# An adaptive-layernorm attention block: the gate's matmuls threaded into the K and V matmuls, and the scores placed ahead of V

## The chip, the core and the metric

The kernel runs on one core of a Trainium2 chip. The core has a matrix engine (TensorE, PE in the profile, with its weight loads listed apart as PEld), a vector engine (DVE), a scalar engine for activations (ACT), a general engine (POOL) and a synchronisation engine (SP) that issues most of the transfers. The engines run side by side, each through its own list of instructions in a fixed order, and wait for one another on semaphores. Matmuls write into eight accumulation banks (PSUM), from which DVE or ACT copy the results into the on-chip memory (SBUF). The metric is the device time of one execution in microseconds (us).

## What is computed

```python
def reference(x, c, wqkv, wo, w_mod):
    B, N, D = x.shape                      # 2, 256, 1152
    mod = (_silu(c) @ w_mod).reshape(B, 6, 1, D)
    shift_a, scale_a, gate_a, ... = [mod[:, i] for i in range(6)]
    h = _layernorm(x, axis=-1) * (1 + scale_a) + shift_a
    qkv = h @ wqkv
    q, k, v = ...
    p = _softmax(jnp.einsum('bqd,bkd->bqk', q, k) * D ** (-0.5), axis=-1)
    a = jnp.einsum('bqk,bkd->bqd', p, v) @ wo
    return x + gate_a * a
```

All tensors are bf16. Three of the six modulation vectors are used: shift, scale and gate. The gate multiplies the columns of the projected attention, so it can equally be multiplied into the columns of `wo`, once for each batch, and this kernel does that.

## The kernel before

The 512 rows (2 batches of 256) form four row tiles of 128, numbered 0 to 3; tiles 0 and 1 are batch 0, tiles 2 and 3 batch 1. The 1152 features form nine blocks of 128, numbered j. A small scheduler (`Sched`) notes what each operation reads and writes, derives the semaphore waits from that, and emits the operations of every engine in the order in which the program lists them. So the order of the lines is the order of each engine's queue, and nothing is reordered later. PSUM banks are handed out by `get_bank` (line 287), the least recently taken first; a matmul that starts in a bank waits until the bank's last contents have been read.

The stages, in the order of the program:

- Transfers: x, then the shift and scale columns of `w_mod` (tile `wmss`), the weights of Q, the gate columns (`wmg`), the weights of K, of V, and `wo` (into `woG[:, 0]`). All are issued at the start, nearly all from SP.
- Statistics and normalisation of x on DVE and ACT, while TensorE multiplies silu(c) (`cTs`, padded to 128 columns, two of which carry data) with `wmss`, in five chunks of up to 512 columns (`mod_ss_j`). Between those matmuls it transposes the normalised rows block by block (`xn_transposes_j`), through two banks in turn; every transposed block is copied to `hT[:, j]` by the engine that the list `raw_evict_eng` (line 475) names.
- The shift and scale rows are copied to `modsb` (line 488 on), transposed into columns by 18 transposes of two rows (line 496 on), and turned into per-partition scalars (`modT_group`), with which `modulate` (line 514) scales and shifts each block of `hT`.
- Q and K (`qk_group`, line 528): groups of five and four output blocks, each a bank that accumulates over nine matmuls of 512 columns. ACT copies them to `qkT`. Between them stand `mod_gate` (line 552), the gate's 27 matmuls in the same form as those for shift and scale, and `gate_bcast_and_woG` (line 561). This spreads each batch's gate row over all 128 partitions by multiplying with a selector (`sel`), copies the result to `gateb`, and has DVE multiply `wo` with it, first into `woG[:, 1]` and then in place in `woG[:, 0]`.
- V (`v_tile`, line 541): four row tiles, each in three banks (512, 512 and 128 columns); ACT copies them to `v_sb`.
- Attention: `scores`, `evict_scores` (ACT), `dve_chain` (scale, row maximum, subtraction), `exp_tile` (ACT), `finalize` (division by the row sum), `pT_of` (transposing the probabilities), `av_of` (attention times V, with the copies to `aT` alternating between ACT and DVE), and `proj`, which multiplies with `woG`, adds x on DVE and sends each chunk of the output off. The last lines (649 to 666) fix their order: scores of all four tiles with the softmax of batch 0 between them, then batch 0 up to its projection, then batch 1.

Before the loop over `xn`, a one-element `Exp` on ACT (line 453) brings in the exponential's table early.

Of the kernel before, what the change touches and what calls it, by code (L numbers as in the profile page):

```python
# [5 lines left out]
DT = mybir.dt  # L6
# [174 lines left out]
def bass_standalone__dit_adaln_block__diffusion_kernel(  # L181
# [70 lines left out]
    MPAD = 128  # L252
    cTs = salloc("cTs", [P, DC, MPAD], DT.bfloat16)
    modsb = salloc("modsb", [B, 3 * D], DT.bfloat16)
    modT = salloc("modT", [P, 2 * DC, B], DT.float32)
    onep16 = salloc("onep16", [P, DC, B], DT.bfloat16)
# [22 lines left out]
    pT = salloc("pT", [P, B, 2, N], DT.bfloat16, at=xn_off + 2 * NT * N * 2)  # L279
    assert 2 * NT * N * 2 + B * 2 * N * 2 <= NT * D * 2  # L280

    pb = [nc.alloc_psum_tensor(f"pb{i}", [P, 512], DT.float32) for i in range(8)]
    pb16 = [pb[i][:, :].bitcast(DT.bfloat16) for i in range(8)]

    lru = list(range(8))

    def get_bank(exclude=()):
        for i, b in enumerate(lru):
            if b not in exclude:
                lru.pop(i)  # L290
                lru.append(b)
                return b
        raise RuntimeError("no psum bank")

    def dma(dst, src, eng="sp", name=None):
# [3 lines left out]
    def mm(dst, lhsT, rhs, start, stop):  # L299
        return S.add("pe", lambda e: e.matmul(dst, lhsT, rhs, start=start, stop=stop),  # L300
                     reads=[lhsT, rhs], writes=[dst])

    def tp(dst, src, ident_ap):
        return S.add("pe", lambda e: e.transpose(dst, src, ident_ap),  # L304
                     reads=[src, ident_ap], writes=[dst])
# [51 lines left out]
    def alt(a="act", b="dve"):  # L357
        rr[0] ^= 1
        return a if rr[0] else b
# [28 lines left out]
    for k3 in range(3):  # L388
# [8 lines left out]
          reads=[ident[:]], writes=[ident[:]])  # L397
    S.add("pool", lambda e: e.memset(cTs[:], 0.0), writes=[cTs[:]])
    S.add("pool", lambda e: e.memset(sel[:], 1.0), writes=[sel[:]])
    S.add("pool", lambda e: e.affine_select(sel[:], sel[:], pattern=[[-1, B], [0, P]],  # L400
# [51 lines left out]
    act(xn[:, 3, :], xn[:, 3, :], ACT.Copy, scale_=rden[:, 3:4])  # L452
    act(rs1[:, 0:1], ve16[:, 0:1], ACT.Exp)
    for i in (0, 1, 2):
# [7 lines left out]
    def mod_ss_j(j):  # L462
        for k, (c0, w) in enumerate(ss_chunks):
            mm(pb[ss_banks[k]][0:MPAD, 0:w], cTs[:, j, :], wmss[:, j, c0:c0 + w],
               start=(j == 0), stop=(j == DC - 1))

    tp_banks = [get_bank(exclude=ss_banks), get_bank(exclude=ss_banks)]

    def xn_transposes_j(j, evict_eng):
# [3 lines left out]
        copy(evict_eng, hT[:, j, :], pb16[bk][:, 0:T])  # L473

    raw_evict_eng = ["dve", "dve", "act", "dve", "dve", "act", "dve", "dve", "act"]
    bk_w = get_bank(exclude=ss_banks)
# [5 lines left out]
    for kind, j in pre_order:  # L482
        if kind == "m":
            mod_ss_j(j)
        else:
            xn_transposes_j(j, raw_evict_eng[j])

    ev_order = [(0, "dve"), (2, "act"), (1, "act"), (3, "dve"), (4, "dve")]
    for k, eng in ev_order:
        c0, w = ss_chunks[k]  # L490
        copy(eng, modsb[0:2, c0:c0 + w], pb[ss_banks[k]][0:2, 0:w])

    xn_transposes_j(7, raw_evict_eng[7])
    JA = 3
    mps = {}
    for (j0, j1) in ((0, JA), (JA, DC)):
        bk_t = get_bank()
        n = j1 - j0
        view = pb16[bk_t][:, 0:2 * n * B].rearrange("p (m b) -> p m b", b=B)
        mps[(j0, j1)] = view  # L500
        for jj in range(j0, j1):
            for m, r in ((jj, jj - j0), (DC + jj, n + jj - j0)):
                tp(view[:, r, :], modsb[0:2, m * P:(m + 1) * P], ident[0:2, 0:2])
    xn_transposes_j(8, raw_evict_eng[8])

# [21 lines left out]

    def qk_group(t3, cols):
        banks = [get_bank() for _ in cols]
        for j in range(DC):  # L530
            for ci, cc in enumerate(cols):
                mm(pb[banks[ci]][:, 0:T],
                   wq[:, j, t3 * D + cc * P:t3 * D + (cc + 1) * P],
                   hT[:, j, :], start=(j == 0), stop=(j == DC - 1))
        for ci, cc in enumerate(cols):
            idx = t3 * DC + cc
            copy("act", qkT[:, idx, :], pb[banks[ci]][:, 0:T])

    v_chunks = [(0, 512), (512, 512), (1024, 128)]

    def v_tile(i):
        banks = [get_bank() for _ in v_chunks]
        for j in range(DC):
            for k, (c0, w) in enumerate(v_chunks):
                mm(pb[banks[k]][:, 0:w], hT[:, j, i * P:(i + 1) * P],
                   wq[:, j, 2 * D + c0:2 * D + c0 + w], start=(j == 0), stop=(j == DC - 1))
        for k, (c0, w) in enumerate(v_chunks):
            copy("act", v_sb[:, i, c0:c0 + w], pb[banks[k]][:, 0:w])

    g_chunks = [(0, 512), (512, 512), (1024, 128)]  # L550

    def mod_gate():
        banks = [get_bank() for _ in g_chunks]
        for j in range(DC):
            for k, (c0, w) in enumerate(g_chunks):
                mm(pb[banks[k]][0:MPAD, 0:w], cTs[:, j, :], wmg[:, j, c0:c0 + w],
                   start=(j == 0), stop=(j == DC - 1))
        for k, (c0, w) in enumerate(g_chunks):
            copy("dve", modsb[0:2, NSS + c0:NSS + c0 + w], pb[banks[k]][0:2, 0:w])

    def gate_bcast_and_woG():
        for b in range(B):
            gbanks = [get_bank() for _ in g_chunks]
            for k, (c0, w) in enumerate(g_chunks):
                mm(pb[gbanks[k]][:, 0:w], sel[:, b, :], modsb[0:2, NSS + c0:NSS + c0 + w],
                   start=True, stop=True)
            for k, (c0, w) in enumerate(g_chunks):
                copy("dve", gateb[:, b, c0:c0 + w], pb[gbanks[k]][:, 0:w])
        for b in (1, 0):
            gview = bass.AP(tensor=gateb, offset=b * D, ap=[[B * D, P], [0, DC], [1, D]])  # L570
            src = woG[:, 0, :, :]
            dst = woG[:, b, :, :]
            S.add("dve", lambda e, dst=dst, src=src, gview=gview: e.tensor_tensor(  # L573
                dst, src, gview, op=ALU.mult),
                  reads=[src, gateb[:, b, :]], writes=[dst])

    qk_group(0, [0, 1, 2, 3, 4])
    qk_group(0, [5, 6, 7, 8])
    mod_gate()
    qk_group(1, [0, 1, 2, 3, 4])  # L580
    gate_bcast_and_woG()
    qk_group(1, [5, 6, 7, 8])
    for i in range(NT):
        v_tile(i)

# [28 lines left out]

    def pT_of(b):
# [6 lines left out]
        copy("act", pT[:, b, 0, :], pb16[pt_banks[0]][:, 0:N])  # L622
        copy("dve", pT[:, b, 1, :], pb16[pt_banks[1]][:, 0:N])

    def av_of(b):
        for j in range(DC):
            bk = get_bank()
            for kt in range(2):
                mm(pb[bk][:, 0:N], v_sb[:, 2 * b + kt, j * P:(j + 1) * P],
                   pT[:, b, kt, :], start=(kt == 0), stop=(kt == 1))  # L630
            copy(alt(), aT[:, j, b * N:(b + 1) * N], pb[bk][:, 0:N])

# [3 lines left out]
    def proj(i, last=False):  # L636
        b, qt = divmod(i, 2)
        ob = outsb[:, i, :]
        for k, (c0, w) in enumerate(o_chunks):
# [24 lines left out]
    av_of(1)  # L664
    proj(2)
    proj(3, last=True)

# [30 lines left out]
```

## Time and profile before

| | us |
|---|---|
| median of six executions | 116.92 |
| lowest and highest of them | 115.56 and 118.42 |
| the profiled execution, its own time | 116.94 |
| its span, from the first to the last instruction | 115.2 |
| TensorE busy in the span | 101.6 |
| DVE busy | 54.2 |
| ACT busy | 37.3 |

The granted clock of TensorE over the span was 0.985 of full speed. In the profile, a row gives the source line, the engine, the operation, the tiles written and read, the shape, the number of instructions, and busy time and mean duration. Where a helper records an operation its line is the helper's: 300 is any matmul, 304 any transpose, 309 a copy on ACT, 311 a copy on DVE, 316 a DVE operation with a scalar. So the tiles' names tell the groups apart. A matmul's duration in a row is its latency; consecutive ones overlap, and their spacing has to be taken from the starts. The lists of waits name the instruction whose end released the waiting engine.

### The profile page before, as it was taken

The page shows a single profiled execution, that of the slowest core. Times are in us where ns is not written, and L with a number is a line of the kernel's source. Part 1 is how long each engine was busy: PE and PEld are TensorE (multiplying, and loading weights), DVE is VectorE, ACT ScalarE, POOL GpSimd, SP SyncE. Part 2 cuts the span into 40 slices and gives each one's busy share as a digit, 9 for nine tenths or more (in the row PEclk, how much of TensorE's full clock was granted, in tenths as well). Part 3 has the DMA queues.
Part 4 walks back from the last instruction along what each step waited for, and adds up shares of the span by engine and source line. Part 5 has one row for each costly group of instructions (what it writes and reads, how often), then busy time and mean ns, then how long its engine had stood idle before and what let it go on. Part 6 is the DMA issues. An engine that isn't in the chain of part 4 may idle for free.

```text
span 115.2 us, 1521 instructions
## 1 busy us (share of the span) xinstructions
PE 101.6 (88%) x596; PEld 52.3 (45%) x605; DVE 54.2 (47%) x142; ACT 37.3 (32%) x76; POOL 2.4 (2%) x10
## 2 busy tenths in 40 slices
PE   1728998939999999999989999999997899989990
PEld 1202445523444445544434445555575645574550
DVE  0369884699940000500099999000017577384332
ACT  2933694533008015000350073142157650051000
POOL 6100000000000000000000000000000000000000
PEclk9998699999999999999999999999999999999999
DMA  3999999999999999994000000000000001310131
GB/s 106 330 413 422 413 410 385 361 353 386 393 393 390 394 390 391 390 393 166 0 0 0 0 3 6 0 0 0 0 0 0 6 0 48 100 57 0 59 95 57
DMA packets 10811, 21.04 MB, mean 183 GB/s; under 512 B 1202, under 2 KB 4530, under 8 KB 10804
## 3 DMA queue, kind: packets, MB, share of 16 engines
q1 hardware_dynamic: 10368, 20.32, 48.0%
q10 hardware_dynamic: 436, 0.63, 1.5%
q8 instruction: 5, 0.08, 0.3%
q14 instruction: 2, 0.02, 0.0%
HBM read 19.76 MB, written 1.18 MB: 182 GB/s over the span
## 4 chain that ended last, share of the span: by engine, by line
PE 73%; DVE 9%; DMA 7%; ACT 5%; issue 1%; SPq 1%; DVEq 0%
PE pb L300 72%; DMA wmss<-in_w_mod_dram 7%; DVE hT L316 3%; ACT qkT L309 2%; PE pb L304 2%; DVE modsb L311 1%; ACT v_sb L309 1%; SPq L296 1%; DVE sc_92 L316 1%; DVE smax L339 1%; ACT pT L309 1%; DVE hT L311 1%; DVE outsb L322 1%; ACT hT L309 1%; ACT esb L334 0%
## 5 line engine op out<-in xcount | busy, mean ns | idle before, releaser
L300 PE MATMUL pb<-hT,wq 128*128 128x512 bf16 x159 | 35.5, 379 | 2.2 <-DVE hT L316 1.7
L300 PEld LDWEIGHTS pb<-hT,wq 128*128 128x128 bf16 x162 | 15.5, 98 | 21.2 <-DVE hT L316 2.5
L309 ACT ACTIVATE qkT<-pb 128x512 bf16<-128x512 f32 x18 | 9.2, 605 | 30.1 <-PE pb L300 30.1
L300 PE MATMUL pb<-wq,hT 128*128 128x512 bf16 (+1 forms) x106 | 17.6, 325 | 0.1
L300 PE MATMUL pb<-woG,aT 128*128 128x512 bf16 (+1 forms) x106 | 17.4, 325 | 0.1
L300 PE MATMUL pb<-wmss,cTs 128*128 128x512 bf16 (+1 forms) x44 | 11.2, 404 | 2.8 <-DVE stats L420 2.5
L300 PEld LDWEIGHTS pb<-woG,aT 128*128 128x128 bf16 x108 | 9.2, 98 | 8.5
L300 PEld LDWEIGHTS pb<-wq,hT 128*128 128x128 bf16 x108 | 9.1, 98 | 8.6
L573 DVE TENSOR_TENSOR woG<-woG,gateb 128x10368 bf16<-128x10368 bf16 x2 | 11.1, 5558 | 0.1
L322 DVE TENSOR_TENSOR outsb<-pb,xs 128x512 bf16<-128x512 f32 (+1 forms) x12 | 6.2, 553 | 8.3 <-PE pb L300 8.3
L311 DVE CAST modsb<-pb 2x512 bf16<-2x512 f32 (+2 forms) x6 | 3.1, 559 | 14.4 <-PE pb L300 14.4
L309 ACT ACTIVATE v_sb<-pb 128x512 bf16<-128x512 f32 (+1 forms) x12 | 5.0, 491 | 12.1 <-PE pb L300 12.1
L300 PEld LDWEIGHTS pb<-wmss,cTs 128*128 128x128 bf16 x45 | 4.4, 107 | 9.2 <-DVE stats L420 3.3
L316 DVE TENSOR_SCALAR sc_92<-sc_92 128x256 bf16<-128x256 bf16 x4 | 0.9, 222 | 14.1 <-ACT sc_92 L309 14.1
L311 DVE CAST gateb<-pb 128x512 bf16<-128x512 f32 (+1 forms) x6 | 2.9, 548 | 8.8 <-PE pb L300 8.8
L420 DVE BATCH_NORM_STATS2 stats<-xs 128x6 f32<-128x384 bf16 x9 | 4.4, 541 | 1.9 <-DMA xs<-in_x_dram 1.9
L300 PE MATMUL pb<-pT,v_sb 128*128 128x256 bf16 x36 | 4.3, 273 | 0.8 <-ACT pT L309 0.8
L316 DVE TENSOR_SCALAR hT<-hT,modT 128x256 bf16<-128x256 bf16 x18 | 4.8, 284 | 0.5
L334 ACT ACT_TABLE_LOAD x3 | 3.8, 1283 | 2.3 <-issue 2.2
L300 PE MATMUL pb<-wmg,cTs 128*128 128x512 bf16 (+1 forms) x26 | 4.5, 324 | 0.1
L311 DVE CAST aT<-pb 128x256 bf16<-128x256 f32 x9 | 3.8, 425 | 1.3 <-PE pb L300 1.2
L300 PE MATMUL pb<-qkT 128*128 128x256 bf16 x36 | 4.1, 272 | 0.0
(76 smaller groups left out, 65.4 us busy)
## 6 DMA issues: line engine op xcount, KB each, us to landing
wmss<-in_w_mod_dram SPq DMA_DIRECT2D x9, 576.0 KB, 10.1
wq<-in_wqkv_dram SPq DMA_DIRECT2D x6, 864.0 KB, 14.2
wmg<-in_w_mod_dram SPq DMA_DIRECT2D x3, 864.0 KB, 10.6
woG<-in_wo_dram SPq DMA_DIRECT2D x3, 864.0 KB, 14.0
wq<-in_wqkv_dram SPq DMA_DIRECT2D x3, 480.0 KB, 14.8
wq<-in_wqkv_dram SPq DMA_DIRECT2D x3, 384.0 KB, 9.5
out_dram<-outsb SPq DMA_DIRECT2D x8, 128.0 KB, 1.7
xs<-in_x_dram SPq DMA_DIRECT2D x2, 288.0 KB, 4.1
```

Of the source, the lines that this page charges most:

```text
L296: return S.add(eng, lambda e: e.dma_start(dst, src), reads=[src], writes=[dst], is_dma=True, own_sem_name=name)
L300: return S.add("pe", lambda e: e.matmul(dst, lhsT, rhs, start=start, stop=stop), reads=[lhsT, rhs], writes=[dst])
L304: return S.add("pe", lambda e: e.transpose(dst, src, ident_ap), reads=[src, ident_ap], writes=[dst])
L309: return S.add("act", lambda e: e.activation(dst, src, ACT.Copy), reads=[src], writes=[dst])
L311: return S.add(eng, lambda e: e.tensor_copy(dst, src), reads=[src], writes=[dst])
L316: return S.add(eng, lambda e: e.tensor_scalar(dst, src, a1, None, op0=op0), reads=rd, writes=[dst])
L322: return S.add(eng, lambda e: e.tensor_tensor(dst, a, b, op=op), reads=[a, b], writes=[dst])
L334: return S.add("act", lambda e: e.activation(dst, src, func, bias=bias, scale=scale_, accum_out=accum_out), reads=rd, writes=wr)
L339: return S.add(eng, lambda e: e.tensor_reduce(dst, src, axis=AX.X, op=op), reads=[src], writes=[dst])
L420: S.add("dve", lambda e, i=i, k3=k3: e.bn_stats(stats[:, i, k3, :], xs[:, i, k3 * LNC:(k3 + 1) * LNC]), reads=[xs[:, i, k3 * LNC:(k3 + 1) ...
L573: S.add("dve", lambda e, dst=dst, src=src, gview=gview: e.tensor_tensor(dst, src, gview, op=ALU.mult), reads=[src, gateb[:, b, :]], writes ...
```

## The change

The change has these parts.

- Bank bookkeeping: `mm` records which banks have an accumulation under way, and `get_bank` passes over those. `use_bank` takes a named bank; the transposes of shift and scale get two named ones.
- Start: other engines evict some transposed blocks (block 2 on DVE, block 7 on ACT), the copy of block 5 is put behind the copies of shift and scale, shift and scale are multiplied in the chunk order 0, 2, 1, 3, 4, and the transposes of block 7 come behind those of shift and scale. The one-element `Exp` moves behind Q's first group.
- Gate: 81 matmuls of two columns replace the 27. The stationary operand is now a 128x128 block of `wmg`, the moving one the two data columns of `cTs`, and one of them follows each of K's 81 matmuls. They give the gate as columns, in one bank (`bk_g`). `gate_finish` copies them to scalars and builds 18 tiles of 128x128 on DVE by adding a scalar to a zero tile `zt`; multiplying these with the identity spreads the gate (`gate_bcast_interleave`), threaded into V's second and third tile. `woG_scaling` follows V's third tile in the program.
- Attention: the scores of all tiles and the whole softmax stand ahead of V, in the tile order 2, 3, 0, 1. Batch 1 then goes first to its projection, with the copies of the probabilities and of `aT` on DVE alone, and batch 0 follows. The last output tile has four chunks (512, 256, 256, 128), sent from SP and ACT in turn.

```diff
@@ salloc
+    modsb_off = cursor[0]
     modsb = salloc("modsb", [B, 3 * D], DT.bfloat16)
+    gT16 = salloc("gT16", [P, DC, B], DT.bfloat16)
+    gT32 = salloc("gT32", [P, DC, B], DT.float32)
+    zt = salloc("zt", [P, P], DT.bfloat16)
...
+    gtile = salloc("gtile", [P, NGB, P], DT.bfloat16, at=modsb_off)
...
+    open_banks = set()
     def get_bank(exclude=()):
         for i, b in enumerate(lru):
-            if b not in exclude:
+            if b not in exclude and b not in open_banks:
...
+    S.add("pool", lambda e: e.memset(zt[:], 0.0), writes=[zt[:]])
...
-    act(rs1[:, 0:1], ve16[:, 0:1], ACT.Exp)
...
-        for k, (c0, w) in enumerate(ss_chunks):
+        for k in (0, 2, 1, 3, 4):
+            c0, w = ss_chunks[k]
...
-    raw_evict_eng = ["dve", "dve", "act", "dve", "dve", "act", "dve", "dve", "act"]
+    raw_evict_eng = ["dve", "dve", "dve", "dve", "dve", "act", "dve", "act", "act"]
...
-            xn_transposes_j(j, raw_evict_eng[j])
+            xn_transposes_j(j, raw_evict_eng[j], defer=(j == 5))
...
-    xn_transposes_j(7, raw_evict_eng[7])
+    flush_raw()
...
-        bk_t = get_bank()
+        bk_t = use_bank(bk_w if j0 == 0 else ss_banks[0])
...
+    xn_transposes_j(7, raw_evict_eng[7])
     xn_transposes_j(8, raw_evict_eng[8])
...
                 mm(pb[banks[ci]][:, 0:T], ...)
+                if interleave:
+                    interleave()
...
+    def gate_interleave():
+        if gidx[0] >= len(gate_mms):
+            return
+        if bk_g[0] is None:
+            bk_g[0] = get_bank()
+        ech, kj = gate_mms[gidx[0]]
+        gidx[0] += 1
+        mm(pb[bk_g[0]][:, 2 * ech:2 * ech + 2], wmg[:, kj, ech * P:(ech + 1) * P],
+           cTs[:, kj, 0:B], start=(kj == 0), stop=(kj == DC - 1))
...
+    def gate_finish():
+        while gidx[0] < len(gate_mms):
+            gate_interleave()
+        gps = pb[bk_g[0]][:, 0:2 * DC].rearrange("p (e b) -> p e b", b=B)
+        copy("dve", gT32[:], gps)
+        copy("dve", gT16[:], gT32[:])
+        copy("dve", gT32[:], gT16[:])
+        for n, (b, ech) in enumerate(gb_list):
+            tsc("dve", gtile[:, n, :], zt[:, :], gT32[:, ech, b:b + 1], None, ALU.add)
...
+    def gate_bcast_interleave():
...
+        key = (b, ech // 4)
+        if key not in gb_banks:
+            gb_banks[key] = get_bank()
+        bk = gb_banks[key]
+        c0 = (ech % 4) * P
+        mm(pb[bk][:, c0:c0 + P], gt, ident[:, :], start=True, stop=True)
+        if ech % 4 == 3 or ech == DC - 1:
+            e0 = (ech // 4) * 4 * P
+            w = c0 + P
+            copy("dve", gateb[:, b, e0:e0 + w], pb[bk][:, 0:w])
...
     qk_group(0, [0, 1, 2, 3, 4])
+    act(rs1[:, 0:1], ve16[:, 0:1], ACT.Exp)
     qk_group(0, [5, 6, 7, 8])
-    mod_gate()
-    qk_group(1, [0, 1, 2, 3, 4])
-    gate_bcast_and_woG()
-    qk_group(1, [5, 6, 7, 8])
-    for i in range(NT):
-        v_tile(i)
+    qk_group(1, [0, 1, 2, 3, 4], interleave=gate_interleave)
+    qk_group(1, [5, 6, 7, 8], interleave=gate_interleave)
+    gate_finish()
...
+        chunks = [(0, 512), (512, 256), (768, 256), (1024, 128)] if last else o_chunks
...
-            eng = "act" if (last and k == len(o_chunks) - 1) else "sp"
+            eng = "act" if (last and k % 2 == 1) else "sp"
...
+    scores(2); evict_scores(2)
+    scores(3); evict_scores(3)
+    dve_chain(2); exp_tile(2)
     scores(0); evict_scores(0)
+    dve_chain(3); exp_tile(3)
     scores(1); evict_scores(1)
+    finalize(2, 3)
     dve_chain(0); exp_tile(0)
-    scores(2); evict_scores(2)
     dve_chain(1); exp_tile(1)
-    scores(3); evict_scores(3)
     finalize(0, 1)
-    pT_of(0)
+    v_tile(0)
+    v_tile(1, interleave=gate_bcast_interleave)
+    v_tile(2, interleave=gate_bcast_interleave)
+    woG_scaling()
+    v_tile(3)
+    pT_of(1, engs=("dve", "dve"))
+    av_of(1, eng="dve")
+    proj(2)
+    proj(3)
+    pT_of(0, engs=("act", "dve"))
     av_of(0)
-    dve_chain(2); exp_tile(2)
-    dve_chain(3); exp_tile(3)
-    finalize(2, 3)
     proj(0)
-    proj(1)
-    pT_of(1)
-    av_of(1)
-    proj(2)
-    proj(3, last=True)
+    proj(1, last=True)
```

More of the change, by code (lines that the diff above doesn't have):

```diff
@@ L280, in bass_standalone__dit_adaln_block__diffusion_kernel @@
     assert 2 * NT * N * 2 + B * 2 * N * 2 <= NT * D * 2
+    NGB = B * DC
+    gtile = salloc("gtile", [P, NGB, P], DT.bfloat16, at=modsb_off)
+    assert NGB * P * 2 <= 3 * D * 2
     pb = [nc.alloc_psum_tensor(f"pb{i}", [P, 512], DT.float32) for i in range(8)]
@@ L293, in get_bank, with use_bank @@
         raise RuntimeError("no psum bank")
+    def use_bank(b):
+        lru.remove(b)
+        lru.append(b)
+        return b
     def dma(dst, src, eng="sp", name=None):
@@ L299, in mm @@
     def mm(dst, lhsT, rhs, start, stop):
+        bk = nc.lookup_mloc(dst.tensor).bank
+        if start:
+            assert bk not in open_banks, f"psum bank {bk}: accumulation group already open"
+            open_banks.add(bk)
+        else:
+            assert bk in open_banks, f"psum bank {bk}: accumulate into a closed group"
+        if stop:
+            open_banks.discard(bk)
         return S.add("pe", lambda e: e.matmul(dst, lhsT, rhs, start=start, stop=stop),
@@ L467, in bass_standalone__dit_adaln_block__diffusion_kernel, with xn_transposes_j @@
     tp_banks = [get_bank(exclude=ss_banks), get_bank(exclude=ss_banks)]
-    def xn_transposes_j(j, evict_eng):
+    def xn_transposes_j(j, evict_eng, defer=False):
         bk = tp_banks[j % 2]
@@ L472, in xn_transposes_j, with flush_raw @@
             tp(pb16[bk][:, i * P:(i + 1) * P], xn[:, i, j * P:(j + 1) * P], ident[:, :])
-        copy(evict_eng, hT[:, j, :], pb16[bk][:, 0:T])
-    raw_evict_eng = ["dve", "dve", "act", "dve", "dve", "act", "dve", "dve", "act"]
+        if defer:
+            deferred_raw.append((bk, j, evict_eng))
+        else:
+            copy(evict_eng, hT[:, j, :], pb16[bk][:, 0:T])
+    def flush_raw():
+        for bk, j, eng in deferred_raw:
+            copy(eng, hT[:, j, :], pb16[bk][:, 0:T])
+        deferred_raw.clear()
+    raw_evict_eng = ["dve", "dve", "dve", "dve", "dve", "act", "dve", "act", "act"]
+    deferred_raw = []
     bk_w = get_bank(exclude=ss_banks)
@@ L526, in bass_standalone__dit_adaln_block__diffusion_kernel, with qk_group @@
         modulate(j)
-    def qk_group(t3, cols):
+    def qk_group(t3, cols, interleave=None):
         banks = [get_bank() for _ in cols]
@@ L539, in bass_standalone__dit_adaln_block__diffusion_kernel, with v_tile @@
     v_chunks = [(0, 512), (512, 512), (1024, 128)]
-    def v_tile(i):
+    def v_tile(i, interleave=None):
         banks = [get_bank() for _ in v_chunks]
@@ L546, in v_tile @@
                    wq[:, j, 2 * D + c0:2 * D + c0 + w], start=(j == 0), stop=(j == DC - 1))
+                if interleave:
+                    interleave()
         for k, (c0, w) in enumerate(v_chunks):
             copy("act", v_sb[:, i, c0:c0 + w], pb[banks[k]][:, 0:w])
[L550 to L568, printed above, removed]
+    bk_g = [None]
+    gate_mms = []
+    for ech in range(DC):
+        for kj in range(DC):
+            gate_mms.append((ech, kj))
@@ new lines, in bass_standalone__dit_adaln_block__diffusion_kernel @@
+    gidx = [0]
+    def gate_interleave():
[7 more added lines that the diff above has]
+           cTs[:, kj, 0:B], start=(kj == 0), stop=(kj == DC - 1))
+    gb_list = [(b, ech) for b in range(B) for ech in range(DC)]
+    def gate_finish():
[7 more added lines that the diff above has]
+            tsc("dve", gtile[:, n, :], zt[:, :], gT32[:, ech, b:b + 1], None, ALU.add)
@@ new lines, in bass_standalone__dit_adaln_block__diffusion_kernel @@
+    gbi = [0]
+    gb_banks = {}
+    def gate_bcast_interleave():
+        if gbi[0] >= len(gb_list):
+            return
+        b, ech = gb_list[gbi[0]]
+        n = gbi[0]
+        gbi[0] += 1
+        gt = gtile[:, n, :]
+        key = (b, ech // 4)
[8 more added lines that the diff above has]
+            copy("dve", gateb[:, b, e0:e0 + w], pb[bk][:, 0:w])
@@ L569, in gate_bcast_and_woG, with woG_scaling @@
+    def woG_scaling():
+        while gbi[0] < len(gb_list):
+            gate_bcast_interleave()
         for b in (1, 0):
@@ L613, in finalize, with pT_of @@
             tsc("dve", esb[:, i, :], esb[:, i, :], srec[:, i:i + 1], None, ALU.mult)
-    def pT_of(b):
+    def pT_of(b, engs=("act", "dve")):
         pt_banks = [get_bank(), get_bank()]
@@ L621, in pT_of, with av_of @@
                    esb[:, i, kt * P:(kt + 1) * P], ident[:, :])
-        copy("act", pT[:, b, 0, :], pb16[pt_banks[0]][:, 0:N])
-        copy("dve", pT[:, b, 1, :], pb16[pt_banks[1]][:, 0:N])
-    def av_of(b):
+        copy(engs[0], pT[:, b, 0, :], pb16[pt_banks[0]][:, 0:N])
+        copy(engs[1], pT[:, b, 1, :], pb16[pt_banks[1]][:, 0:N])
+    def av_of(b, eng=None):
         for j in range(DC):
@@ L630, in av_of @@
                    pT[:, b, kt, :], start=(kt == 0), stop=(kt == 1))
-            copy(alt(), aT[:, j, b * N:(b + 1) * N], pb[bk][:, 0:N])
+            copy(eng or alt(), aT[:, j, b * N:(b + 1) * N], pb[bk][:, 0:N])
     o_chunks = [(0, 512), (512, 512), (1024, 128)]
@@ L638, in proj @@
         ob = outsb[:, i, :]
-        for k, (c0, w) in enumerate(o_chunks):
+        chunks = [(0, 512), (512, 256), (768, 256), (1024, 128)] if last else o_chunks
+        for k, (c0, w) in enumerate(chunks):
             bk = get_bank()
```

## The prediction

> **What bounds the kernel now.** I read the busy table and the slices first, then the chain of waits, then the span cut into stages, then single rows.
>
> ```profile
> PE 101.6 (88%) x596; PEld 52.3 (45%) x605; DVE 54.2 (47%) x142; ACT 37.3 (32%) x76; POOL 2.4 (2%) x10
> ...
> PE   1728998939999999999989999999997899989990
> PEld 1202445523444445544434445555575645574550
> DVE  0369884699940000500099999000017577384332
> ...
> DMA  3999999999999999994000000000000001310131
> ...
> PE 73%; DVE 9%; DMA 7%; ACT 5%; issue 1%; SPq 1%; DVEq 0%
> ```
>
> TensorE holds the path: full from slice 9 on, with dips near slices 29 to 31 and 35. Input transfers end in slice 18 (53 us), so nothing after that waits for one. DVE is idle from slice 13 and full again in slices 20 to 24. The stages, cut at first matmuls:
>
> ```profile
> 25.66:43.17 17.51, 17.39 (x80) 7.69 (x81) 6.91 (x31) 4.31 (x9) 0.00 (x0) 1.00 1.06 390
> 43.17:47.55 4.38, 4.33 (x27) 2.25 (x27) 0.07 (x1) 1.61 (x4) 0.00 (x0) 1.00 1.06 393
> 47.55:57.36 9.81, 9.76 (x46) 4.31 (x46) 1.41 (x3) 0.76 (x2) 0.00 (x0) 1.00 0.59 220
> 57.36:58.72 1.36, 1.15 (x7) 0.44 (x7) 0.94 (x2) 1.36 (x4) 0.00 (x0) 1.00 0.00 0
> 58.72:66.78 8.06, 7.96 (x37) 3.54 (x38) 7.99 (x7) 0.89 (x2) 0.00 (x0) 1.00 0.00 0
> 66.78:84.33 17.55, 17.45 (x108) 9.06 (x109) 5.07 (x1) 5.46 (x14) 0.00 (x0) 1.00 0.00 1
> 84.33:90.14 5.81, 4.57 (x42) 3.65 (x40) 2.96 (x11) 4.12 (x12) 0.00 (x0) 1.00 0.00 0
> ```
>
> First number: us. They are Q, gate, K's first five columns, the gate's spreading, K's last four, V, and scores to the first attention-times-V matmul. The 81 matmuls of Q take 17.51 us, 216 ns apiece from start to start (their rows say 379 because they overlap); by the same spacing a 256-column matmul costs 109 and a 128-column one 56 ns. TensorE has no idle time to fill in Q, K or V, so interleaving hides nothing by itself; what counts is how many nanoseconds of array time are put in and taken out, and which handoffs become exposed.
>
> **The gate computation.** Taken out: the 27 gate matmuls, 4.38 us, and the spreading stage, 1.36 us, of which six matmuls are 4 x 216 + 2 x 56 = 0.98 and the rest waits for ACT to free banks; K's last four then lost 8.06 - 36 x 0.216 = 0.28. From Q to V it was 66.78 - 25.66 = 41.12 us, against 162 x 0.216 = 34.99 for the pure matmuls. So 6.13 us go.
>
> Put in: 81 pairs of a 128x128 weight load and a matmul of two columns, one behind each K matmul. No such sequence is in the trace. Nearest rows:
>
> ```profile
> 23.16 0.45 PE L304 MATMUL pb<-ident,modsb 2*128 2x2 bf16 x12 [0.21 <-ACT modsb L309]
> ```
>
> ```profile
> L304 PE MATMUL pb<-ident,xn x36: 219/219/229, 17.0 to 23.7; 128*128 128x128 bf16 x36
> ```
>
> Twelve two-column matmuls, each with its own load of 128 columns, start within 0.45 - 0.16 (the length of the last) = 0.29 us: 26 ns a pair. Those loads are only two rows deep. For full ones the second row helps: 229 instead of 219 ns is a matmul that followed a stall and had no earlier matmul to hide its load, so a bare 128x128 load costs some 10 ns, and a 26 ns matmul covers it. Lower bound nothing (if the pairs slip under their neighbours), upper bound 98 ns, the row of a full load. I take 26: 81 x 0.026 = 2.1 us. [...] Net Q to V: -6.13 + 2.1 = -4.0 us. The sequencer is no limit: four instructions per 242 ns here, against the scores' two per 109 already sustained.
>
> **Scores before V, spreading inside V, DVE reordered.** Call T the end of the last K matmul. Before, the first attention-times-V matmul started 90.14 - 66.78 = 23.36 us after T. Now:
> - Scores meet ACT still evicting the last four K columns (2.06 us for four), formerly behind V: the last lands at about T + 1.5, so the first score tile ends at 1.7 instead of 0.98. Four tiles (36 x 0.109 = 3.93) end at T + 4.65. The softmax's handoff, 5.81 - 3.93 - 0.9 = about 1.0 us of TensorE wait, goes behind V.
> - gate_finish puts three small copies (about 0.2 each with handoff) and 18 tile builds on DVE ahead of the softmax. A 256-column add with a per-row scalar repeats every 0.20 us; the 1152-column one takes 519 ns against 284, 0.26 ns a column, so 128 columns repeat in about 0.17: 3.1 us, done at T + 3.9. Queued behind it are the softmax chains (1.0 us a tile on DVE, 0.6 on ACT), and behind those on ACT the score evictions and V's first; all ends near T + 10.7. V hides it: tile 0 runs from 4.65 to 9.05.
> - Spreading: 18 matmuls of 128 columns in V's second tile, 18 x 56 ns = 1.0 us, loads hidden. The last is in slot 18 of 27, near T + 13.0; DVE's six gate copies (0.68 or 0.28 each) end near T + 13.9. Without V's cover this would add some 2.9 us of DVE time.
> - Banks, by the allocation order: V's third tile receives the three of the second, since the spreading rotates through the other five, so it waits for ACT's three evictions (1.25 us): about 0.9 us. TensorE then reaches the transposes at T + 24.1 and, with the usual 0.9 for their handoff, attention-times-V at T + 25.0.
> - DVE's two scalings of the output weights (5.56 us each) formerly ran in 60.70 to 71.85, far ahead of use. Now they start at T + 13.9 and end at T + 25.0, and both evictions of the transposed probabilities are queued behind them on DVE: 0.6 us more puts attention-times-V at T + 25.65. DVE sets this, which swallows the bank wait. Against 23.36: +2.29 us.
> - Attention-times-V of batch 1 evicts on DVE alone. Five such copies took 2.17 us, 0.43 each: nine end 4.35 us after its start, while projection wants the ninth by 2.2 + 8 x 0.216 = 3.9. +0.48 us. The other batch keeps both engines.
>
> **Start and end.** Moving the third transposed block's eviction from ACT (0.60) to DVE (0.42) frees its bank 0.24 us sooner, for which the fourth transposes waited (0.47 idle at 19.54). The eviction of block 7 leaves DVE, where it stood from 23.26 until the modulation vectors at 23.59: 0.33. Chunk 2 of shift and scale ready earlier, the deferred block on ACT and the fixed banks only keep ACT from being later than DVE. -0.55 us; bounds 0 and -0.7. The exponential table load (1.28) moves to ACT's idle time after Q's first evictions; the row before has 5 us of idle there. The new 128-column memset on POOL (the like took 0.20) delays only the constant that ACT reads at 5.07 from 3.18 to about 3.4: nothing. SP's input queue is untouched. Output DMAs go in tile order 2, 3, 0, 1, one more in number, with two on ACT's queue at the end, where nothing is behind them. Four chunks in the last tile let the final eviction (0.28) start at once instead of behind a 0.69: -0.1 us.
>
> **Sum.** -0.55 - 4.0 + 2.29 + 0.48 - 0.1 = -1.9 us. The profiled execution took 116.94 us (span 115.2), equal to the median of 116.92, so the forecast is 115.0 us. What a measurement of this kernel can tell from no change is about 1%, 1.2 us.
>
> **Rivals.**
> 1. Weight loads exposed (slower). In the K stage, loads and matmuls of two columns alternate with large ones; if the array cannot fetch the next full weights during 26 ns, each pair costs a load. At 98 ns it is 81 x 0.098 = 7.9 instead of 2.1: 120.8 us. It turns slower above (1.9 + 2.1) / 81 = 49 ns a pair. [...] Against it: the 10 ns of a bare load. Chance 0.17.
> 2. DVE becomes the bound by more than I give it. From the last gate copy to the first attention-times-V it runs without a gap, so each microsecond of lateness there (tile builds at 0.25 each, copies of the spreading late, softmax chain dearer) counts fully. At 1.5 us more: 116.5. For it: DVE already sets T + 25.65; against it: 3 us of slack before the spreading. Chance 0.18.
> 3. The handoffs cost less than computed: attention-times-V at T + 24.1, no stall at the ninth copy. 115.0 - 1.55 - 0.48 = 113.0. For it: TensorE's own work allows it; against it: DVE's 11.1 us cannot start before the spreading ends. Chance 0.09.
>
> **How the numbers follow.** My forecast has 0.56, with a range of its own from 114.1 to 115.9 (the start's bounds and 0 to 35 ns a pair around 26). Faster by over 1% (below 115.75): nearly all of it, 0.53, and rival 3, 0.09: 0.62. Within 1%: the rest of it and most of rival 2: 0.19. Slower: rival 1 and the tail of rival 2: 0.19. The range, 113.4 to 118.0, leaves out most of rival 1 and a third of rival 3.
>
> **What would show it.** K's 81 matmuls take 81 x 242 = 19.6 us; near 25 would be rival 1. Q's first matmul starts near 25.1, K ends near 62. A wait of about 0.7 us in the first score tile on ACT; about 0.9 at V's third tile on ACT's evictions; DVE full from the spreading to the transposed probabilities, with TensorE waiting about 1.5 us there in all. If DVE finishes its scalings before TensorE arrives, the +2.29 is too large; if K is stretched by more than 4 us, the forecast is wrong.

## The result, and the profile after

| | before | after |
|---|---|---|
| median, us | 116.99 (20 executions) | 113.42 (10 executions) |
| lowest and highest | 115.56 and 118.42 | 113.18 and 115.76 |
| profiled execution, own time | 116.94 | 113.38 |
| its span | 115.2 | 111.7 |

The ratio of after to before is 0.974, with a 95% interval from 0.969 to 0.979; it is taken over executions that were not disturbed. The same kernel, measured once more in another session, gave 0.987 (0.982 to 0.993). The gain is clear; its size to half a per cent is not, and the first experiment shows why.

The page of the profile after, parts 1, 2 and 4:

```profile
PE 100.1 (90%) x669; PEld 53.7 (48%) x680; DVE 58.0 (52%) x166; ACT 34.8 (31%) x71; POOL 2.5 (2%) x11
...
PE   0779998859999998999999899998997999989991
...
DVE  0598875899920000000000897789999863373332
...
PE 70%; DVE 17%; DMA 5%; ACT 3%; issue 1%; SPq 1%
PE pb L321 69%; DVE woG L643 10%; DMA wmss<-in_w_mod_dram 5%; DVE hT L337 3%; ACT qkT L330 3%; PE pb L325 2%; DVE modsb L332 1%; DVE hT L332 1%; SPq L309 1%; ACT pT L330 0%; DVE onep_74 L337 0%; DVE onep_75 L332 0%; DVE modT L332 0%; DVE outsb L343 0%; DVE gateb L332 0%
```

DVE has gone from 9% of the chain to 17%, and 10 of those points are one line, the scaling of the output weights, which was not on the chain before. The stages after, cut as before (Q, K with the gate's pairs, scores, V with the spreading, transposes of the probabilities, attention times V of batch 1; the first number after the stretch is its length in us):

```profile
23.90:41.63 17.73, 17.60 (x80) 7.71 (x80) 6.92 (x31) 6.14 (x13) 0.00 (x0) 1.00 1.06 387
41.63:61.42 19.79, 19.25 (x159) 9.75 (x162) 0.00 (x0) 4.51 (x10) 0.00 (x0) 1.00 0.60 221
61.42:66.28 4.86, 4.45 (x39) 3.54 (x39) 4.48 (x25) 2.34 (x7) 0.00 (x0) 1.00 0.01 2
66.28:85.48 19.20, 18.58 (x124) 9.96 (x125) 17.20 (x25) 6.25 (x20) 0.00 (x0) 1.00 0.00 1
85.48:86.80 1.32, 0.39 (x7) 0.21 (x5) 1.32 (x3) 1.18 (x3) 0.00 (x0) 1.00 0.00 0
86.80:88.86 2.06, 2.06 (x18) 1.77 (x19) 1.68 (x6) 0.00 (x0) 0.00 (x0) 1.00 0.00 0
```

Set against before by the places where the stages begin:

| stretch, us | before | after | difference | forecast |
|---|---|---|---|---|
| start of the span to the first transposes of the normalised rows | 17.04 | 15.79 | -1.25 | 0 |
| from there to Q's first matmul | 8.62 | 8.11 | -0.51 | -0.55 |
| Q to the end of K | 41.12 | 37.52 | -3.60 | -4.0 |
| end of K to attention times V | 23.36 | 25.38 | +2.02 | +2.29 |
| from there to the end | 25.06 | 24.86 | -0.20 | +0.38 |
| sum | 115.2 | 111.7 | -3.54 | -1.9 |

Without the first row it is -2.29 us. Of the change only a memset on POOL and the order of the shift and scale chunks lie in that row, both put at nothing in the forecast; the first experiment is about it.

### The profile page after: what moved, and what is told of

It reads as the page before. It is cut to its first block, busy times and chain, and to the rows that moved or that the text cites. A ratio compares the mean times of both kernels' runs of the same rounds, so it can differ in the third digit from the quotient of the medians.

```text
span 111.7 us, 1691 instructions
## 1 busy us (share of the span) xinstructions
PE 100.1 (90%) x669; PEld 53.7 (48%) x680; DVE 58.0 (52%) x166; ACT 34.8 (31%) x71; POOL 2.5 (2%) x11
## 4 chain that ended last, share of the span: by engine, by line
PE 70%; DVE 17%; DMA 5%; ACT 3%; issue 1%; SPq 1%
PE pb L321 69%; DVE woG L643 10%; DMA wmss<-in_w_mod_dram 5%; DVE hT L337 3%; ACT qkT L330 3%; PE pb L325 2%; DVE modsb L332 1%; DVE hT L332 1%; SPq L309 1%; ACT pT L330 0%; DVE onep_74 L337 0%; DVE onep_75 L332 0%; DVE modT L332 0%; DVE outsb L343 0%; DVE gateb L332 0%
## 5 line engine op out<-in xcount | busy, mean ns | idle before, releaser
L321 PE MATMUL pb<-hT,wq 128*128 128x512 bf16 x157 | 36.9, 378 | 1.3 <-DVE hT L337 1.2
L321 PE MATMUL pb<-wq,hT 128*128 128x512 bf16 (+1 forms) x105 | 18.6, 324 | 0.6 <-ACT v_sb L330 0.4
L321 PE MATMUL pb<-woG,aT 128*128 128x512 bf16 (+2 forms) x115 | 17.6, 312 | 0.1
L321 PEld LDWEIGHTS pb<-woG,aT 128*128 128x128 bf16 x117 | 10.1, 98 | 7.7 <-DVE aT L332 0.2
L321 PE MATMUL pb<-cTs,wmg 128*128 128x2 bf16 x81 | 13.3, 164 | 0.5 <-ACT qkT L330 0.3
L321 PE MATMUL pb<-wmss,cTs 128*128 128x512 bf16 (+1 forms) x44 | 11.8, 429 | 0.8 <-DMA wmss<-in_w_mod_dram 0.7
L343 DVE TENSOR_TENSOR outsb<-pb,xs 128x512 bf16<-128x512 f32 (+2 forms) x13 | 6.6, 525 | 10.1 <-PE pb L321 10.1
L321 PEld LDWEIGHTS pb<-cTs,wmg 128*128 128x128 bf16 x81 | 7.7, 95 | 0.8 <-ACT qkT L330 0.8
L332 DVE CAST aT<-pb 128x256 bf16<-128x256 f32 x13 | 4.8, 416 | 1.1 <-PE pb L321 1.0
L321 PEld LDWEIGHTS pb<-pT,v_sb 128*128 128x128 bf16 x36 | 3.4, 98 | 2.1 <-DVE pT L332 1.1
## 6 DMA issues: line engine op xcount, KB each, us to landing
woG<-in_wo_dram SPq DMA_DIRECT2D x3, 864.0 KB, 13.8
```

Of the source, the lines that this page charges most:

```text
L332: return S.add(eng, lambda e: e.tensor_copy(dst, src), reads=[src], writes=[dst])
L343: return S.add(eng, lambda e: e.tensor_tensor(dst, a, b, op=op), reads=[a, b], writes=[dst])
```

## The experiments

In all of them, stretches are read from one profiled execution, and the ratio is to the kernel before in the same session. "From Q to the end" starts at Q's first recorded matmul.

**The changed kernel again, and its start undone.**

> The changed kernel once more, as the yardstick for the others of this call. Theory: of the 1.76 us by which its first Q matmul came earlier than before's, only some 0.5 us belong to the change (from the first transposes of the normalised rows to the first Q matmul, 8.11 us against 8.62); the other 1.25 us is the arrival of the first transfers, which differs from execution to execution, so in some executions of either kernel the first transposes start near 15.8 us and in others near 17 us. Rival: the changed start itself brings the whole 1.76, and the first transposes always start near 15.8 us.

> The changed kernel with the start of before (engines of the evictions, chunk order, order of the transposes, banks, the early exponential). Theory: 8.6 us from the first transposes to the first Q matmul, against 8.1; all later stages as in the changed kernel, 87.8 us from the first Q matmul to the end; 0.5 us slower than the changed kernel, so about 0.978 of before. Rival (the start is worth the whole 1.76): the first transposes at 17 us and 1.8 us slower than the changed kernel.

```diff
-    raw_evict_eng = ["dve", "dve", "dve", "dve", "dve", "act", "dve", "act", "act"]
+    raw_evict_eng = ["dve", "dve", "act", "dve", "dve", "act", "dve", "dve", "act"]
-            xn_transposes_j(j, raw_evict_eng[j], defer=(j == 5))
+            xn_transposes_j(j, raw_evict_eng[j], defer=False)
```

(and the chunk order, the order of the transposes, their banks and the place of the `Exp`). The changed kernel again, by the stages of the execution that was profiled:

```profile
17.30:25.42 8.12, 6.20 (x71) 4.13 (x70) 5.67 (x19) 2.89 (x6) 0.00 (x0) 1.00 1.07 364
25.42:113.20 87.78, 82.31 (x556) 44.87 (x564) 41.60 (x109) 22.70 (x54) 0.00 (x0) 1.00 0.38 136
```

The first transposes came at 17.30 us, later than in the execution of before, with the changed start. From there on everything repeats to 0.02 us: 8.12 and 87.78. So the first stretch differs between executions of one kernel by as much as it differed between the two kernels: in this one the first shift and scale matmul had waited 2.28 us for its weights and started at 8.82 us, in the first profile after 0.75 us and 7.33. That execution took 114.91 us, against 116.94 for the one of before with its first transposes at 17.04: 2.0 us less at nearly the same start. The two traces that hold the old gate both start late (17.04 and 16.66 us), but the kernel before can start early too: an execution of 115.53 us had a span of 113.8, and less the 98.2 from the first transposes on (115.2 - 17.04) that leaves 15.6 us, by estimate.

With the old start, the stretch from the first transposes to Q took 8.72 us, and 8.64 and 8.62 in the two later experiments that keep it: the changed start is worth 0.5 to 0.6. But from Q on this execution needed 89.2 us instead of the 87.8 expected. That is no part of the change either; its slices and its stages from Q to the end of K and from there on show where it lies:

```profile
PEclk9999999985999999999999999999999999999999
```

```profile
24.49:63.45 38.96, 38.36 (x238) 17.94 (x242) 6.92 (x31) 9.03 (x19) 0.00 (x0) 0.96 0.77 284
63.45:113.70 50.25, 45.46 (x320) 27.42 (x323) 34.69 (x78) 12.06 (x34) 0.00 (x0) 1.00 0.08 24
```

The clock granted to TensorE fell to half near 25 us (0.5 in the slice from 25.6 to 28.4 us), 0.4 us after Q's first recorded matmul, and Q to the end of K took 38.96 instead of 37.52 us. From the end of K on, 50.25 us are those of the changed kernel (111.7 - 61.42 = 50.28). The ratio, 0.985 (0.979 to 0.991), cannot be told from the 0.987 of the changed kernel in the same session; the gain of the start is shown by the stretch, not by the times.

**Which wait sets the start of attention times V.**

> The changed kernel, but a V tile never takes the banks of the tile before it. Theory: V's third tile no longer waits 0.9 us for ACT, TensorE reaches the transposes of the probabilities 0.9 us sooner and waits 0.9 us longer there for DVE's second scaling of the output weights; time as the changed kernel within 0.1 us. Rival (TensorE and not DVE sets the start of attention times V): 0.9 us faster than the changed kernel.

```diff
-        banks = [get_bank() for _ in v_chunks]
+        banks = [get_bank(exclude=last_v[0]) for _ in v_chunks]
+        last_v[0] = tuple(banks)
```

> The changed kernel, but DVE scales the output weights of batch 0 only after it has copied batch 1's transposed probabilities, and ACT takes the copies of batch 1's attention times V. Theory: DVE's second scaling is what attention times V waits for in the changed kernel; without it the probabilities are copied as soon as they are transposed, and attention times V starts 24.8 us after the end of K instead of 25.4; 0.6 us faster. Rival (the handoff through DVE itself costs the time, or ACT, busy with V's last eviction, delays the new copies by as much): no gain.

```diff
-    woG_scaling()
+    woG_scaling(bs=(1,))
     v_tile(3)
     pT_of(1, engs=("dve", "dve"))
-    av_of(1, eng="dve")
+    woG_scaling(bs=(0,))
+    av_of(1, eng="act")
```

The handoff in time order, first in the changed kernel, then with V's banks apart, then with the scaling late (start, us, engine, operation; in brackets the idle time before and what ended it):

```profile
80.98 5.56 DVE L643 TENSOR_TENSOR woG<-woG,gateb 128x10368 bf16<-128x10368 bf16 x1
...
85.48 0.39 PE L325 MATMUL pb<-ident,esb 128*128 128x128 bf16 x4
86.46 0.48 DVE L332 COPY pT<-pb 128x256 bf16<-128x256 bf16 x2
...
86.80 2.23 PE L321 MATMUL pb<-pT,v_sb 128*128 128x256 bf16 x18 [0.93 <-DVE pT L332]
```

```profile
80.97 5.56 DVE L646 TENSOR_TENSOR woG<-woG,gateb 128x10368 bf16<-128x10368 bf16 x1
...
84.60 0.39 PE L325 MATMUL pb<-ident,esb 128*128 128x128 bf16 x4
86.44 0.48 DVE L332 COPY pT<-pb 128x256 bf16<-128x256 bf16 x2
...
86.78 0.48 PE L321 MATMUL pb<-pT,v_sb 128*128 128x256 bf16 x2 [1.80 <-DVE pT L332]
```

```profile
87.09 0.39 PE L325 MATMUL pb<-ident,esb 128*128 128x128 bf16 x4
87.46 0.49 DVE L332 COPY pT<-pb 128x256 bf16<-128x256 bf16 x2 [4.90 <-PE pb L325]
...
87.81 2.23 PE L321 MATMUL pb<-pT,v_sb 128*128 128x256 bf16 x18 [0.33 <-DVE pT L332]
```

In the first, DVE's copies begin when its scaling ends, 0.98 us after the transposes started. In the second, TensorE is 0.88 us earlier at the transposes and stands 0.87 us longer: nothing gained, 87.75 us from Q to the end in both. In the third, DVE waits for TensorE instead (4.90 us of idle), and attention times V starts 0.72 us after the transposes instead of 1.32. From Q to the end it took 87.15 us, 0.60 less, as expected. Moving the copies of attention times V to ACT, the other part of that edit, has no share in it: from there to the projection it took 2.06 us in both. The ratios, 0.978 (0.969 to 0.986) and 0.972 (0.966 to 0.977), come from two different sessions and cannot be set against each other.

**The hole at the first gate matmul.**

> The changed kernel, but the bank of the gate's columns is set aside before Q's second group, so that the first gate matmul does not wait for ACT to empty it. Theory: the 0.48 us hole behind K's first matmul goes, all later work moves forward by as much, DVE's spreading and scaling included: 0.5 us faster than the changed kernel. Rival: the hole covers an eviction that is needed anyway and turns up at the fifth matmul or at K's second group; no gain.

```diff
+    bk_g[0] = get_bank()
+    kept.add(bk_g[0])          # get_bank passes over it until gate_finish
     qk_group(0, [5, 6, 7, 8])
```

Waits between 40 and 43 us, in the changed kernel and in this one (the engine that waits, for whom: us in total, times, longest):

```profile
PEld pb L321 <- ACT qkT L330: 0.8, 1, 0.8
PE pb L321 <- ACT qkT L330: 0.3, 1, 0.3
```

```profile
ACT qkT L331 <- PE pb L322: 3.9, 1, 3.9
```

TensorE no longer waits there, and the wait does not turn up elsewhere: the scores wait 0.69 us in all for ACT, in the changed kernel 0.70. From Q to the end it took 87.27 us, 0.48 less. Ratio 0.975 (0.968 to 0.982), against 0.987 for the changed kernel in the same session.

**Form or interleaving.**

> The changed kernel with the 81 two-column gate matmuls in one block behind K instead of one behind each K matmul. Theory: the gain is in the two-column form, not in the interleaving; a pair of a full 128x128 weight load and its matmul costs 25 to 26 ns in a row as well, so the block takes 2.1 us; the 0.48 us wait for the gate's bank goes, and ACT's last K evictions are over before the scores begin, so that the output weights are scaled some 0.3 us earlier: 0.8 us faster than the changed kernel. Rival (a full load hides only behind a large matmul): 56 to 98 ns a pair, a block of 4.5 to 7.9 us, 2 to 5 us slower.

```diff
-    qk_group(1, [0, 1, 2, 3, 4], interleave=gate_interleave)
-    qk_group(1, [5, 6, 7, 8], interleave=gate_interleave)
+    qk_group(1, [0, 1, 2, 3, 4])
+    qk_group(1, [5, 6, 7, 8])
```

In the changed kernel, three of K's matmuls and the pairs between them:

```profile
44.56 0.38 PE L321 MATMUL pb<-hT,wq 128*128 128x512 bf16 x1
44.77 0.16 PE L321 MATMUL pb<-cTs,wmg 128*128 128x2 bf16 x1
44.80 0.38 PE L321 MATMUL pb<-hT,wq 128*128 128x512 bf16 x1
45.01 0.16 PE L321 MATMUL pb<-cTs,wmg 128*128 128x2 bf16 x1
45.04 0.38 PE L321 MATMUL pb<-hT,wq 128*128 128x512 bf16 x1
```

K's matmuls are 0.24 us apart here, against 0.216 in Q. The block and the first score matmul in time order:

```profile
59.86 2.17 PE L321 MATMUL pb<-cTs,wmg 128*128 128x2 bf16 x81
...
61.89 0.27 PE L321 MATMUL pb<-qkT 128*128 128x256 bf16 x1
```

From the first pair to the first score matmul it is 61.89 - 59.86 = 2.03 us for 81 pairs, 25 ns each, with a fresh 128x128 load in every one and no large matmul between. The rival is out. The form makes the gain; the threading adds nothing that TensorE could use. The scores take 4.14 us instead of 4.86, as ACT is done by then. The whole moved by 0.40 us (87.35), not by 0.8. DVE sets the start of attention times V here too, and its first scaling began 51.08 us after Q's first matmul, against 51.49: 0.41 earlier and no more. TensorE lost its further lead at the spreading matmuls, where it stood 0.77 us for banks that ACT had not yet emptied. The ratio is 0.978 (0.972 to 0.983).

**The parts alone, on the kernel before.**

> The kernel before with only the new order of attention: scores and softmax ahead of V, tiles 2, 3, 0, 1, batch 1 first, its copies on DVE; gate and start as before. Theory: the hidden handoff of the softmax (1.0 us) is paid back by the scores' wait for ACT's last K evictions (0.7) and by small handoffs; 23.2 us from the end of K to attention times V against 23.4: 0.2 us faster than before. Rival (the order is where the change gains): at least 1 us faster.

> The kernel before with only the new gate: two-column matmuls behind K's, tiles on DVE, spreading inside V's second and third tile, scaling behind it; start and order of attention as before. Theory: 37.5 us from the first Q matmul to the end of K against 41.1 (-3.6), V longer by the spreading (1.0) and by the bank wait (0.9), softmax not held up: 1.7 us faster than before. Rival (the new gate needs the new order, since DVE's scalings meet the softmax): the softmax starts 2 us later and the gain is gone.

For the first, the last lines of the program were replaced by the new ones, without the gate's calls; for the second, V and the spreading were put ahead of the scores, and the old start and the old last lines kept. The order alone: 41.12 us from Q to the end of K, 23.01 to attention times V (before 23.36), 89.28 from Q to the end against 89.54. Ratio 0.998 (0.993 to 1.004): no gain that can be measured. The gate alone: 89.26 us from Q to the end, in an execution in which the clock again fell at Q's beginning (a mean of 0.96 from Q to the end of K, in 38.96 us, as above; 37.52 without). Less these 1.44 us it is 87.82, 1.72 less than before; the ratio is 0.983 (0.976 to 0.990). The parts, -0.5 for the start, -0.26 for the order and -1.72 for the gate, make -2.5, near the -2.29 of the whole. So the new gate does not need the new order, as its rival had it.

**Together.**

> The changed kernel with the gate's bank set aside, V's banks kept apart and the second scaling behind the copies of the probabilities, all three together. Theory: the V tile's bank wait was hidden only by DVE's scaling, so with the scaling moved it counts too: 0.49 + 0.60 + 0.88 = 2.0 us less from the first Q matmul to the end, 85.8 us against 87.75. Rival (a third engine, ACT with V's evictions, holds the copies up next): 86.7 us, no more than the sum of the two that gained alone.

> The changed kernel with V's banks kept apart, the second scaling moved, and the gate's 81 pairs in one block behind K. Theory: TensorE alone sets the time from Q on, so the scores' wait for ACT, which the block covers (0.72 us), now counts as well: 87.75 - 0.49 - 0.72 - 0.60 - 0.88 = 85.1 us from the first Q matmul to the end. Rival (DVE, later by the gate's tiles, takes over again, as it did with the block alone): 85.8 us or more.

> As the one before, with five idle 512-column matmuls into an unused bank between the last transposes and Q, where TensorE otherwise waits 1.4 us for DVE. Theory: the half-clock windows of 3.4 us that some executions show behind such a wait (Q then takes 1.44 us longer) do not come there any more: no execution with Q longer than 17.6 us, and fewer with a mean clock of 0.985. Rival (the windows come from the waits nearer the beginning): as many of them as without. In either case Q does not start later by more than 0.1 us.

> The changed kernel and nothing but the five idle matmuls between the last transposes and Q. Theory: the wait of TensorE in front of Q is what lets the clock fall to half for one window in some executions; filled, no execution shows a mean clock of 0.985, where 6 of 17 executions of the changed kernel did; the times spread less, and from Q to the end it takes 87.75 us as before the filling. Rival (the windows belong to the waits near the beginning, and six executions without one were chance): two executions in six at 0.985.

The last two add this behind the transposes of block 8:

```diff
+    for k in range(5):
+        mm(pb[lru[0]][:, 0:512], ident[:, :], xs[:, 0, 0:512], start=True, stop=True)
```

| | first transposes to the end, us | ratio | executions with a mean clock of 0.985 |
|---|---|---|---|
| changed kernel | 95.87 | 0.974 and 0.987 | 6 of 17 |
| three repairs | 93.93 | 0.964 (0.955 to 0.972) | 1 of 6 |
| block and two repairs | 94.01 | 0.961 (0.952 to 0.971) | 3 of 6 |
| the same, filled | 94.02 | 0.960 (0.954 to 0.966) | 0 of 6 |
| changed kernel, filled | 95.93 | 0.976 (0.970 to 0.982) | 0 of 6 |

The stretch starts at the first transposes here, since the record of Q's first matmul is missing in some of these traces. Three repairs bring 1.94 us, the 2.0 of the theory: the bank wait, worth nothing alone, is worth 0.86 (1.94 less 0.48 and 0.60) once DVE's scaling is out of the way. With the block it should have been 0.7 more, and was not. In that kernel, in time order:

```profile
70.97 0.42 ACT L355 ACTIVATE esb<-sc 128x256 bf16<-128x256 bf16 x1 [0.40 <-DVE sc L337]
...
71.39 1.23 ACT L330 ACTIVATE v_sb<-pb 128x512 bf16<-128x512 f32 x3
...
72.01 0.10 PEld L321 LDWEIGHTS pb<-ident,gtile 128*128 128x128 bf16 x1 [0.58 <-ACT v_sb L330]
...
72.50 0.10 PEld L321 LDWEIGHTS pb<-ident,gtile 128*128 128x128 bf16 x1 [0.38 <-ACT v_sb L330]
```

V begins earlier than the softmax can follow; ACT's evictions of V's first tile stand behind the exponentials, those behind DVE's chains, and the spreading matmuls wait for the banks. The rival expected of that kernel came true, through ACT's queue. The filled version of it has the lowest median of all, 111.57 us; by its ratio it cannot be told from the two rows above it.

## Why the prediction was right, and where not

T is the end of K, as in the prediction.

- *The gate's pairs at 26 ns, 2.1 us in all.* Right: the spacing of K's matmuls is 241 ns with a pair between, 25 ns more than the 216 of Q, 2.0 us in all, and 25 ns in a block, with loads 128 rows deep where the 26 came from loads of two rows. Rival 1, with 98 ns a pair, falls with it; that 128-column matmuls with a full load each start 56 ns apart already spoke against it.
- *Q to the end of K, -4.0.* It was -3.60. Missing was a term: the gate's bank was one of Q's second group, not yet emptied, and TensorE stood 0.48 us behind K's first matmul. The banks of V were followed through the allocation order; that of the gate was not. Setting it aside gave the 0.48 back.
- *The scores' wait for ACT, 0.7 us; the softmax hidden behind V; V's third tile waiting 0.9 us for banks.* Right: 0.70 us in two steps, DVE free for the gate copies at T + 10.35 (forecast 10.7), and 0.86 us at V's third tile.
- *DVE sets the start of attention times V.* Right, and shown from both sides: the bank wait removed brought nothing, the scaling moved brought 0.60. The scalings ended at T + 25.1 (forecast 25.0), attention times V at T + 25.38 (25.65).
- *The nine copies on DVE, +0.48.* Wrong by its whole size: the ninth copy ended 3.59 us after attention times V began (forecast 4.35), before the projection's ninth matmul at 3.79. The 0.43 us a copy was read from a group that alternated with ACT's and was paced by TensorE; nine in a row took 3.07 us, 0.33 from start to start with a duration of 0.41. A busy time that includes a producer's pace is no rate of the engine.
- *The start, -0.55, the four chunks at the end, -0.1.* -0.51 in the pair of profiles, -0.5 to -0.6 with the start undone. The last row of the stages is -0.20, so without the +0.48 the end is within 0.1 of its forecast.
- *The order of attention.* Its gain was given as 1.0 us hidden against 0.7 for the scores' wait; alone it made 0.26 us, and the new gate without it came to 87.82 us by estimate, against 87.75 with it (the start is outside that stretch): the change would have been much the same without the new order.

The forecast of -1.9 us stands against -2.29 where the change acts, and in part by luck: the 0.48 us of the gate's bank, left out, and the 0.48 of the nine copies, put in, cancel. The rest of the difference between 115.0 and the 113.42 measured is mostly the 1.25 us of the first stretch, which the sum took from one execution of the kernel before as if it were fixed. It was luck too that the median still lies in the range given, 0.02 us above its lower end of 113.4 and below the 114.1 to 115.9 of the prediction's main case. The lower end of that case does not follow from the bounds it names: pairs that cost nothing would alone give 115.0 - 2.1 = 112.9. The fastest executions of the two kernels in the result, 115.56 and 113.18 us, are 2.38 apart, close to the 2.29.

## What to carry to other kernels

For a product with few output columns, try the large matrix as the stationary operand, in whatever place: here 512, 256 and 128 moving columns took 216, 109 and 56 ns, two took 25 with a full weight load in each, and so 81 pairs (2.0 us) were cheaper than 27 large matmuls (4.4 us). When work is moved behind a long instruction of an engine (here two copies of the probabilities behind DVE's scaling of 5.56 us, which cost 0.60 us), look for what stands behind it there and who waits for that; a second wait hidden under it (here 0.86 us) is worth repairing only together with it. Before a stage time is used as a base, see how much of it is an arrival that differs from execution to execution.

## What the runs showed of the hardware that was not expected

In the kernel before, the granted clock of TensorE was 0.50 of full speed from 10.4 to 13.8 us, a window of 3.4 us, and 1.00 on both sides of it; over the span that makes the mean of 0.985 (1 - 0.5 x 3.4 / 115.2). Five of the fourteen traces show one such window, all five with this mean: in the other four, spans of 110.4 to 114.6 us, it was 3.3 to 3.4 us long by the same sum, an estimate. Where the window fell decided what it cost. In the kernel before, the order alone and the three repairs it lay between 10 and 14 us; in the kernel before, the normalised rows, which the first transposes need, were complete only at 16.80 us, and those transposes began at 17.04, so it cost little. With the start undone and in the gate alone it began at about 25 us, after TensorE had waited 1.7 us for Q's first block; with the start undone, the longest matmul of Q and K lasted 631 ns (389 in the changed kernel, with a median of 379 in both), and the window cost 1.44 us. A wait of 1.72 us stands in front of Q in the kernel before too, and one of 1.7 in the order alone, both with a clock of 1.00 from Q to the end of K, so the wait alone does not decide.

The clock row does not tell everything. In the profile after it shows full speed throughout, yet the shift and scale matmuls of 512 columns started 427 ns apart up to 12.8 us and 216 ns apart from then on. In the kernel before they started 216 ns apart from 8.9 us on and 427 from 10.3 to 13.9. So a mean of 0.985 against 1.000 does not say that the kernel before was at a disadvantage there.

Five idle matmuls in front of Q cost nothing (95.93 against 95.87 us), and 0 of 12 executions then had a mean clock of 0.985, where the changed kernel without them had 6 of 17, and all runs with the changed start and no filling 21 of 53. These counts speak for the filling, but how it would act stays open: in none of the eight traces with the changed start and no filling does a window lie at Q, and the one window among them lies ahead of the place of the filling. Where the windows fell in the executions that were not profiled is not known.
